# Longer estimated durations for the attention's matmuls, and a smaller allowance for array-mode changes, in the list schedule of an attention and MoE kernel on one Trainium2 core

## The chip, the cores and the metric

One core of one Trainium2 chip runs the whole kernel. The metric is the device time of one execution in microseconds, the median of several runs. Beside those runs there is one profiled execution, from which the trace comes.

## The reference

```
q_d, k_d, v_d = means over 4 neighbouring positions of q, k, v     # [4, 8, 144, 64] each
out_d     = softmax(q_d k_d^T / 8) v_d                             # coarse, global
out_up    = repeat(out_d, 4, axis=positions)
out_local = softmax(mask(q k^T / 8, |i - j| < 4)) v                # q, k, v: [4, 8, 576, 64]
x   = (out_up + out_local) as [2304, 512]
h   = x @ w_in                                                     # [512, 1024]
s   = h * softmax(h)
ln  = (s - mean(s)) / sqrt(var(s) + 1e-6) * g
x   = ln @ w_out                                                   # [1024, 512]
h2  = x @ w2_in                                                    # [512, 2048]
out = (h2 * cos(h2)) @ w2_out                                      # [2048, 512]
```

## The kernel before

The work falls into three parts that overlap. **Attention** goes over 4 batches, each in blocks of 192 positions and pairs of heads. The local part (class Loc) masks and scores with `ls` (L590 the mask, L592 the scores, three of 70 columns), makes a softmax (L475 to L482, the exponential L478 on ScalarE), transposes with `lt` (L600), copies on ScalarE (L602), and multiplies with the values, `lv` (L613, twelve small products for one block, 64 columns of the array wide). The global part (Glob) does the same on pooled positions: `gs` (L537, 64 rows by 64 columns of the array), `gt` (L548), `gv` (L559, 64 columns wide). **The first MoE layer** takes 128 tokens at a time: `h` is a product over w_in (h1_half), its maximum is L644, L655 to L659 make the softmax product and thereby free the bank of h, and ln_t transposes with `lnT` (L679) before x2 multiplies with w_out into `x`. **The second layer** has a plain start (plain_h, plain_o, 256 tokens) and then four groups of 512 tokens (quad_h, quad_o) by a Strassen-like scheme of seven products for each m from 0 to 7, into the banks s1, s26, s57 and s34; the names with numbers, as s26_6096, are those of one m (s26_5991 is m = 4, s26_6096 m = 5, s26_6201 m = 6, s26_6306 m = 7 of the first group; their cosines work in a_6041, a_6146, a_6251 and a_6356). VectorE sums the products (L981 to L988), the cosine runs through ScalarE and VectorE (L871, L873, L875, L876, L878), and its split into two parts (L387 hi on ScalarE, L388 lo on VectorE) gives GR, with which PE makes `oa` and `ob`.

All large products are made of three f32r products (mm3, L395 to L397) of a number split in a high and a low part by split (L387, L388). Four of the seven products of each m (the S products; the other three are plain) need S_h and S_l, sums of quarters of w2_in. combine(m) builds them in two half steps, each through the same buffer: a load from DRAM (L886), four sums on VectorE (L888 to L891), and a split, L387 on ScalarE to S_h and L388 on VectorE to S_l. w2o_step and wload bring the other weights; loads are issued by SP.

What sets the order is not the code's order. Each instruction is recorded as a Step with an estimated duration (Step.estimate, L110), connect finds what depends on what, and arrange (L201) makes a list schedule for all engines: forwards simulates the engines with these durations and takes at each turn the ready step with the earliest due time, backwards sets due times from the result, and of 20 rounds the order with the earliest estimated end is kept and fixed on every engine's queue. MODE_SWITCH (L50) is added on PE where the next matmul uses another width of the array than the last (Step.mode, L121); pick may also take a step of the same mode that is due up to PATIENCE later. 100 idle matmuls (L718) are due never, so they stand where the plan sees nothing else ready on PE.

Of the kernel before, what the change touches and what calls it, by code (L numbers as in the profile page):

```python
# [46 lines left out]
WRITTEN = {"DVE": 127.0, "Activation": 143.0, "Pool": 127.0}  # L47
DMA_ISSUE, DMA_START, DMA_END, DMA_RATE, DMA_FLIGHT = 475.0, 1100.0, 935.0, 250.0, 8
CLOCK_TICK, CLOCK_COLUMNS = 10240 / 3, 3060.0
MODE_SWITCH, PATIENCE = 150.0, 1200.0  # L50
NEVER = 1e18


# [18 lines left out]
def columns(o):  # L72
    n = 1
    for _, c in list(o.ap)[1:]:
        n *= c
    return n


def width(o):
    return next(z for b, z in (("64", 8), ("32", 4), ("16", 2), ("8", 1)) if b in str(o.dtype))  # L80
# [18 lines left out]
class Step:  # L99
# [10 lines left out]
    def estimate(self, psum):  # L110
        out, n, kind = self.outs[0], columns(self.outs[0]), self.x.opcode
        if self.dma:
            self.bytes = n * list(out.ap)[0][1] * width(out)
            return DMA_START + self.bytes / DMA_RATE + DMA_END
        wide = max([n] + [columns(o) for o in self.ins[:1]])
        if self.engine == "PE":
            d = str(self.ins[0].dtype)
            passes = 1 if "float32r" in d or "bf" in d else 2 if n == 128 else 4
            self.count = passes * n * list(self.ins[0].ap)[0][1] / 128

            self.mode = tuple(64 if list(o.ap)[0][1] <= 64 else 128 for o in (self.ins[0], out))  # L121
            if "float32r" in d:
                return 11.0 + 0.426 * max(n, 256)
            if self.mode[1] == 64:

                return 2.0 + 0.65 * max(n, 60)
            return 5.0 + passes * n / 2.4
        if self.engine == "Activation":
            at = 52 if self.ins[0].bass_ap.tensor.name in psum else 94
            return at + 0.833 * wide + (186 if len(self.outs) > 1 else 0)  # L130
        if self.engine == "DVE":
            full = [o for o in self.ins if columns(o) == n]
            if "TensorScalar" in kind and len(full) == 1 and n >= 256:
                return 65 + 0.535 * n + (110 if len(self.ins) > 1 else 0)
            return 65 + 1.045 * wide
        if self.engine == "Pool":
            return 464 if wide == 1 else 245 + (1.73 if kind == "TensorTensor" else 3.4 if "Ptr" in kind else 0.4) * wide
        return 60.0
# [943 lines left out]
```

## Time and profile before

| | us |
|---|---|
| median of 3 runs | 777.99 (777.79 to 779.13) |
| the profiled execution | 776.28 |
| its span, first to last instruction | 774.5 |
| PE busy (matmuls) | 751.2 |
| VectorE (DVE) busy | 625.7 |
| ScalarE (ACT) busy | 453.2 |

PE is TensorE, PEld its loading of weights, DVE is VectorE, ACT ScalarE, POOL GpSimd, SPq the queue on which SP issues transfers. A time at the start of a row counts from the first instruction of the span. A busy time of PE holds modelled ends, so the spacing of two matmuls is read from their starts. One score (L592) and one product of lv, gs or gv leave two records each in the trace; a transpose and an f32r product leave one.

### The profile page before, as it was taken

The page shows a single profiled execution, that of the slowest core. Times are in us where ns is not written, and L with a number is a line of the kernel's source. Part 1 is how long each engine was busy: PE and PEld are TensorE (multiplying, and loading weights), DVE is VectorE, ACT ScalarE, POOL GpSimd, SP SyncE. Part 2 cuts the span into 40 slices and gives each one's busy share as a digit, 9 for nine tenths or more (in the row PEclk, how much of TensorE's full clock was granted, in tenths as well). Part 3 has the DMA queues.
Part 4 walks back from the last instruction along what each step waited for, and adds up shares of the span by engine and source line. Part 5 has one row for each costly group of instructions (what it writes and reads, how often), then busy time and mean ns, then how long its engine had stood idle before and what let it go on. Part 6 is the DMA issues. An engine that isn't in the chain of part 4 may idle for free.

```text
span 774.5 us, 14770 instructions
## 1 busy us (share of the span) xinstructions
PE 751.2 (97%) x5444; PEld 648.6 (84%) x5444; DVE 625.7 (81%) x1435; ACT 453.2 (59%) x1060; POOL 19.3 (2%) x38
## 2 busy tenths in 40 slices
PE   6999999999999999999999999799999999999998
PEld 4667688888879788888988898698898889888896
DVE  5999999999886778889688998877678677787673
ACT  2656776646663735545567665565557565566544
POOL 3000000000100000000000000000000000000000
PEclk9999999999999999999999999999999999999999
DMA  9998655486763225556553533223211331113201
GB/s 249 275 250 239 190 154 164 130 218 187 224 207 126 75 77 162 159 163 199 187 139 101 154 110 95 69 69 123 69 41 48 130 94 44 41 54 110 55 28 55
DMA packets 82168, 101.85 MB, mean 132 GB/s; under 512 B 26128, under 2 KB 55088, under 8 KB 82096
## 3 DMA queue, kind: packets, MB, share of 16 engines
q1 hardware_dynamic: 82096, 100.91, 44.7%
q8 instruction: 43, 0.70, 0.4%
q14 instruction: 29, 0.24, 0.1%
HBM read 83.58 MB, written 17.30 MB: 130 GB/s over the span
## 4 chain that ended last, share of the span: by engine, by line
PE 69%; DVE 17%; DMA 6%; ACT 4%; issue 2%; POOL 1%; SPq 0%; POOLq 0%; DVEq 0%; ACTq 0%
PE s L395 5%; PE s L397 5%; PE s L396 5%; PE ls L592 3%; PE h L395 3%; PE h L396 3%; PE h L397 3%; PE x L395 3%; PE x L396 3%; PE oa L397 3%; PE x L397 3%; PE oa L395 3%; PE ob L395 3%; PE oa L396 3%; PE ob L396 3%; PE ob L397 3%
## 5 line engine op out<-in xcount | busy, mean ns | idle before, releaser
L395 PE MATMUL x<-P,R 128*128 128x256 f32 x288 | 81.2, 285 | 1.0 <-ACT P L387 0.6
L396 PE MATMUL x<-P,R 128*128 128x256 f32 x288 | 81.2, 283 | 0.5 <-DVE P L388 0.3
L397 PE MATMUL x<-P,R 128*128 128x256 f32 x288 | 80.9, 283 | 0.0
L395 PE MATMUL s<-R 128*128 128x256 f32 x256 | 71.5, 284 | 1.4 <-ACT R L387 1.0
L396 PE MATMUL s<-R 128*128 128x256 f32 x256 | 71.6, 282 | 0.5 <-DVE R L388 0.5
L397 PE MATMUL s<-R,S_l 128*128 128x256 f32 x256 | 70.9, 282 | 0.0
L395 PE MATMUL h<-R,P 128*128 128x512 f32 x144 | 60.7, 421 | 1.2 <-DVE e L659 1.2
L397 PE MATMUL h<-R,P 128*128 128x512 f32 x144 | 59.7, 415 | 0.0
L396 PE MATMUL h<-R,P 128*128 128x512 f32 x144 | 59.3, 412 | 0.1
L478 ACT ACTIVATE le<-ls,sm 128x70 f32<-128x70 f32 x144 | 44.2, 319 | 23.9 <-DVE X L616 8.1
L395 PEld LDWEIGHTS x<-P,R 128*128 128x128 f32 x288 | 54.0, 188 | 2.3 <-ACT P L387 1.4
L396 PEld LDWEIGHTS x<-P,R 128*128 128x128 f32 x288 | 54.1, 188 | 1.4 <-DVE P L388 1.1
L397 PEld LDWEIGHTS x<-P,R 128*128 128x128 f32 x288 | 54.0, 188 | 0.3
L396 PE MATMUL s<-R,w2i 128*128 128x256 f32 x192 | 54.0, 282 | 0.0
L397 PE MATMUL s<-R,w2i 128*128 128x256 f32 x192 | 53.9, 281 | 0.0
L395 PE MATMUL s<-R,w2i 128*128 128x256 f32 x192 | 53.8, 282 | 0.0
L387 ACT ACTIVATE GR<-a 128x1024 fp32r<-128x1024 f32 (+1 forms) x40 | 39.1, 978 | 21.0 <-DVE a L878 20.9
L395 PEld LDWEIGHTS s<-R 128*128 128x128 f32 x256 | 48.0, 189 | 3.1 <-ACT R L387 1.6
L875 ACT ACTIVATE a<-a 128x1024 f32<-128x1024 f32 (+1 forms) x40 | 38.9, 972 | 19.8 <-DVE a L873 19.6
L396 PEld LDWEIGHTS s<-R 128*128 128x128 f32 x256 | 48.6, 190 | 1.6 <-DVE R L388 0.9
L397 PEld LDWEIGHTS s<-R,S_l 128*128 128x128 f32 x256 | 48.2, 190 | 0.2
L388 DVE TENSOR_TENSOR GR<-a,GR 128x1024 fp32r<-128x1024 f32 (+1 forms) x40 | 44.6, 1114 | 2.8 <-ACT GR L387 2.4
(167 smaller groups left out, 2200.0 us busy)
## 6 DMA issues: line engine op xcount, KB each, us to landing
wo<-drw SPq DMA_DIRECT2D x80, 256.0 KB
X<-in_w2o_dram SPq DMA_DIRECT2D x32, 256.0 KB
wr<-in_w2i_dram SPq DMA_DIRECT2D x32, 256.0 KB
lv<-in_vl_dram SPq DMA_DIRECT2D x48, 105.0 KB
kt<-in_k_dram SPq DMA_DIRECT2D x8, 594.0 KB
kw<-in_k_dram SPq DMA_DIRECT2D x24, 198.0 KB
qt<-in_q_dram SPq DMA_DIRECT2D x8, 576.0 KB
diag<-in_q_dram SPq DMA_DIRECT2D x48, 96.0 KB
```

What stands on the lines that cost most here:

```text
L387: nc.scalar.activation(out=hi, in_=src, func=AF.Copy)
L388: nc.vector.tensor_tensor(out=lo, in0=src, in1=hi.bitcast(F32), op=ALU.subtract)
L395: nc.tensor.matmul(ps, lh, rh, start=start, stop=False)
L396: nc.tensor.matmul(ps, lh, rl, start=False, stop=False)
L397: nc.tensor.matmul(ps, ll, rh, start=False, stop=stop)
L478: nc.scalar.activation(out=e[:, j, :], in_=src[:, j, :], func=AF.Exp, bias=neg[:, j:j + 1], scale=scale, accum_out=ssum[:, j:j + 1])
L592: nc.tensor.matmul(ps[:, a * WIN:(a + 1) * WIN], self.d["q"][:, self.h, a].rearrange("p j s -> p (j s)"), self.d["k"][:, self.h, a * QB:a ...
L875: nc.scalar.activation(out=a, in_=a, func=AF.Sin, scale=0.5)
```

## The change

Two estimates of arrange's plan are replaced, and one is split in two; no computation, tile or buffer changes. A product on 64 columns of the array (lv, gs, gv) is estimated at 20 + 0.83 n ns instead of 2 + 0.65 n, with n columns moved and 60 at least. Every other matmul that isn't float32r keeps its estimate where it is bf16; a float32 one is estimated at passes / 2 times the larger of 110 and 3 + n / 1.2 ns, instead of 5 + passes x n / 2.4 (passes is 2 for n = 128, so for the transposes, and 4 else, so for the scores). And the allowance for a change of mode goes from 150 to 80 ns.

```
-MODE_SWITCH, PATIENCE = 150.0, 1200.0
+MODE_SWITCH, PATIENCE = 80, 1200.0
...
             if self.mode[1] == 64:

-                return 2.0 + 0.65 * max(n, 60)
-            return 5.0 + passes * n / 2.4
+                return 20.0 + 0.83 * max(n, 60)
+            if "bf" in d:
+                return 5.0 + n / 2.4
+            return passes / 2 * max(110.0, 3.0 + n / 1.2)
```

In the orders of the changed kernel every line above 128 of the file is two higher (L397 there is L395 before).

PE, in the first MoE layer, the transposes lnT of a_t and the attention around them; before:

```order
L397 MATMUL h_3301<-R_75,P 128x512
L679 MATMUL lnT<-ident,e 128x128 x8
L613 MATMUL lv<-at,lv 64x64 x11
L590 LDWEIGHTS identb
L590 MATMUL ls<-mask,identb 128x210
L592 MATMUL ls<-kw,diag_112 128x70 x3
```

and after:

```order
L399 MATMUL h_3301<-R_75,P 128x512
L681 MATMUL lnT<-ident,e 128x128 x3
L561 MATMUL gv<-at,gvs 64x144 x4
L550 MATMUL gt<-ident,ge 72x128 x3
L681 MATMUL lnT<-ident,e 128x128 x2
L550 MATMUL gt<-ident,ge 72x128 x3
L681 MATMUL lnT<-ident,e 128x128 x3
L592 LDWEIGHTS identb
L592 MATMUL ls<-mask,identb 128x210
L594 MATMUL ls<-kw,diag_112 128x70 x3
```

The eight transposes were in one piece with lv behind them; now gv and gt stand among them, and lv is elsewhere.

VectorE (DVE), in the second layer, the cosine of m = 4 (a_6041), the sums of m = 5 (s26_6096 and following, into hs) and a half step of the combination (the sums of wr with wr, and S_l); before:

```order
L388 TENSOR_TENSOR GR_5112<-a_6041,GR_5112 128x1024
L388 TENSOR_TENSOR w2i10_3926<-wo_6192,w2i10_3926 128x512
L981 TENSOR_TENSOR hs_5113<-s26_6096,hs_5113 128x512
L888 TENSOR_TENSOR wr_3928<-wr_3928 128x128
L889 TENSOR_TENSOR wr_3928<-wr_3928 128x128
L890 TENSOR_TENSOR wr_3928<-wr_3928 128x128
L984 TENSOR_TENSOR hs_5113<-s57_6097,hs_5113 128x512
L891 TENSOR_TENSOR wr_3928<-wr_3928 128x128
L985 TENSOR_TENSOR hs_5113<-s57_6097,hs_5113 128x256
L988 TENSOR_TENSOR hs_5113<-s34_6098,hs_5113 128x512
L388 TENSOR_TENSOR S_l_5111<-wr_3928,R1_75 128x4x128
L873 SCALAR_TENSOR_TENSOR a_6146<-a_6146,hs_5113 128x1024
```

and after:

```order
L890 TENSOR_TENSOR wr_3928<-wr_3928 128x128
L891 TENSOR_TENSOR wr_3928<-wr_3928 128x128
L892 TENSOR_TENSOR wr_3928<-wr_3928 128x128
L390 TENSOR_TENSOR w2i10_3926<-wo_6091,w2i10_3926 128x512
L893 TENSOR_TENSOR wr_3928<-wr_3928 128x128
L880 SCALAR_TENSOR_TENSOR a_6041<-a_6041,wr_3928 128x1024
L390 TENSOR_TENSOR S_l_5111<-wr_3928,R1_75 128x4x128
L983 TENSOR_TENSOR hs_5113<-s26_6096,hs_5113 128x512
L390 TENSOR_TENSOR GR_5112<-a_6041,GR_5112 128x1024
L986 TENSOR_TENSOR hs_5113<-s57_6097,hs_5113 128x512
L390 TENSOR_TENSOR w2i10_3926<-wo_6192,w2i10_3926 128x512
L987 TENSOR_TENSOR hs_5113<-s57_6097,hs_5113 128x256
```

The half step, which began behind the GR of m = 4 and ended behind the last sum of m = 5, now ends ahead of both that GR and the first sum of m = 5.

## Rows read from the trace of the kernel before

**Rows 1.** The page, part 1: busy us (share of the span) and instructions.

```profile
PE 751.2 (97%) x5444; PEld 648.6 (84%) x5444; DVE 625.7 (81%) x1435; ACT 453.2 (59%) x1060; POOL 19.3 (2%) x38
```

**Rows 2.** Stages: length, busy PE, PEld, DVE, ACT, POOL, granted clock, DMA.

```profile
60.00:100.00 40.00, 37.31 (x289) 28.36 (x288) 37.86 (x115) 27.70 (x99) 1.11 (x2) 0.96 0.75 218
180.00:380.00 200.00, 196.21 (x1575) 173.92 (x1574) 160.54 (x495) 106.61 (x317) 9.39 (x12) 1.00 0.51 156
380.00:480.00 100.00, 98.47 (x610) 86.21 (x610) 88.59 (x163) 66.75 (x105) 0.00 (x0) 1.00 0.43 126
480.00:505.00 25.00, 20.73 (x116) 17.82 (x115) 19.52 (x34) 13.94 (x20) 0.00 (x0) 0.93 0.21 64
```

**Rows 3.** Timeline of PE, 255 to 257 us: start, duration, engine, line, what.

```profile
255.35 0.80 PE L592 MATMUL ls<-kw,diag 128*128 128x70 f32 x6
255.96 0.48 PE L396 MATMUL h<-R,P 128*128 128x512 f32 x1
256.28 0.39 PE L397 MATMUL h<-R,P 128*128 128x512 f32 x1
256.51 0.40 PE L395 MATMUL h<-R,P 128*128 128x512 f32 x1
256.84 0.92 PE L613 MATMUL lv<-at,lv 70*64 70x64 f32 x24
```

**Rows 4.** The same from 257.62 us: the last six of those 24 records.

```profile
257.41 0.34 PE L613 MATMUL lv<-at,lv 70*64 70x64 f32 x6
257.69 0.26 PE L590 MATMUL ls<-mask,identb 128*128 128x210 bf16 x1
```

**Rows 5.** Timeline of PE at 250 and at 292 us.

```profile
250.21 1.03 PE L679 MATMUL lnT<-ident,e 128*128 128x128 f32 x8
251.08 0.25 PE L590 MATMUL ls<-mask,identb 128*128 128x210 bf16 x1
...
291.59 1.03 PE L679 MATMUL lnT<-ident,e 128*128 128x128 f32 x8
292.38 0.48 PE L395 MATMUL h<-R,P 128*128 128x512 f32 x1
```

**Rows 6.** Waits of PE, 0 to 310 us: total us, times, longest.

```profile
PE ls L590 <- ACT ge L478: 1.6, 2, 1.0
...
PE h L395 <- DVE e L659: 1.2, 2, 0.6
...
PE ls L590 <- ACT le L478: 0.4, 1, 0.4
```

**Rows 7.** Timeline of DVE, 478 to 503 us; in brackets the idle time before.

```profile
479.49 0.68 DVE L388 TENSOR_TENSOR S_l<-wr,R 128x512 fp32r<-128x512 f32 x1
...
483.14 0.29 DVE L888 TENSOR_TENSOR wr<-wr 128x128 f32<-128x128 f32 x1 [1.15 <-DMA wr<-dra]
...
486.55 0.69 DVE L388 TENSOR_TENSOR w2i<-wo,w2i 128x512 fp32r<-128x512 f32 x1
487.15 0.68 DVE L981 TENSOR_TENSOR wr<-s,wr 128x512 f32<-128x512 f32 x1
487.75 1.22 DVE L388 TENSOR_TENSOR GR<-a,GR 128x1024 fp32r<-128x1024 f32 x1
...
493.55 1.23 DVE L873 SCALAR_TENSOR_TENSOR a<-a,wr 128x1024 f32<-128x1024 int32 x1 [0.93 <-ACT a L871]
...
497.37 1.23 DVE L878 SCALAR_TENSOR_TENSOR a<-a,wr 128x1024 f32<-128x1024 f32 x1 [0.25 <-ACT a L876]
```

**Rows 8.** Timeline of PE, 495 to 504 us.

```profile
496.04 0.28 PE L396 MATMUL s<-R 128*128 128x256 f32 x1
496.16 0.28 PE L397 MATMUL s<-R,S_l 128*128 128x256 f32 x1
499.74 0.54 PE L395 MATMUL oa<-w2i,GR 128*128 128x512 f32 x1 [3.30 <-ACT GR L387]
500.08 0.63 PE L396 MATMUL oa<-w2i,GR 128*128 128x512 f32 x1
500.50 0.63 PE L395 MATMUL oa<-w2i,GR 128*128 128x512 f32 x1
```

## The prediction

> **What bounds the kernel now.** I read the page first, then a table by stage, then the waits, and last the start times where the waits lie. The page shows PE busy for 97% of the span [rows 1]. PE's own work is the bound on the whole, and a new order can win only three things: what PE loses between instructions of different kinds, the few microseconds in which it waits, and stretches at half clock. The stages say where these lie [rows 2]: PE idles 2.69 us from 60 to 100 us, 3.79 from 180 to 380, 1.53 from 380 to 480, and 4.27 us in only 25 us from 480 to 505. From there on the order of every engine soon becomes the same row by row, so nothing is to be had later. VectorE is full from 60 to 100 us (37.86 of 40) and next to it from 380 to 480 (88.59 of 100): where PE waits there, it waits for a chain that runs through VectorE.
>
> **What the change does to the estimates.** Three scores (L592) take from 255.35 to 255.96 us [rows 3], 0.20 us each; the old estimate was 122 ns, the new one is 220. There are 144 of them, so the old plan believed PE some 14 us freer in the attention (144 x 0.098) than the new one does. The first nine of twelve products of L613 start within 0.57 us (256.84 to 257.41) [rows 3, 4], 0.063 each; the old estimate was 44 ns, the new one 73, so the error only changes sign. The allowance: two h products start 0.23 us apart (256.28 to 256.51), and from an h to the first L613 it is 0.33 [rows 3], so entering costs 0.10. Leaving: the last three products start at 257.41, the next instruction at 257.69 [rows 4]; at 0.063 each that leaves 0.09. I take 0.095 for a change either way. 80 ns is nearer to it than 150, a little low.
>
> **Term 1, PE's own order: slower by 1.6 us.** The instructions are the same ones, 100 idle matmuls among them. Counted over the whole order, changes of array width between neighbouring matmuls go from 142 to 152: 10 x 0.095 = +0.95 us. A second thing moves that the plan does not price. Eight transposes of lnT followed by a mask product take 0.87 us to the next start (250.21 to 251.08), and followed by an h product 0.79 (291.59 to 292.38) [rows 5]: a float32 transpose that ends against an f32r product gives 0.08 us back. Such ends (of lnT, lt and gt) go from 64 to 57: 7 x 0.08 = +0.56. Scores that end against an f32r product go from 24 to 22, under 0.1 us. The sum is +1.6, and as PE is full, nothing covers it. Bounds: changes of width at 0.08 give +1.4, at 0.13 +1.9.
>
> The Trainium skill (TensorEngine Tiling (Array Packing), Key Properties) says that a change of the tiling mode drains TensorE. The trace agrees in kind: rows 3 show a loss at the change. The skill's page TensorE: Matmul & The Clock Gate (Single matmul latency) puts the fixed part of one matmul at about 0.17 us; ten changes at that price would be an estimated 1.7 us instead of 0.95, and the sum 0.75 us slower.
>
> **Term 2, the attention's waits: 2.0 us back.** Up to 310 us PE waits 2.0 us in all with a mask product (L590), whose bank a softmax (L478) has not left yet, and 1.2 us for L659 to free the h bank [rows 6]. The first follows from the estimates: scores believed half as long are planned in front of a softmax that in truth is not finished. I take those 2.0 us off. Bounds: nothing (they move elsewhere), and 3.2 with the L659 wait too. I leave that one in, since the first L659 is row 154 of VectorE's order before and row 154 after, at about 62 us, where VectorE is full.
>
> **Term 3, the combination of w2i: 1.6 us back.** From about 383 to 502 us VectorE and ScalarE build S_h and S_l in sixteen half steps through one buffer: a reload (L886), four sums (L888 to L891), a copy on ScalarE (L387), a rest on VectorE (L388, S_l), and only then the next reload. PE needs them in order. In the trace the S_l of the first half for m = 6 starts at 479.49, and L888 of the second half at 483.14, after 1.15 us idle for the reload [rows 7]: a half step wants 3.65 us from one start to the other. Before, only one L873 lies between. After, that S_l stands ahead of L981 of m = 5, and between it and the next L888 lie L981, a GR, L984, a split and L985. With 0.6 us from start to start for S_l, L981, L984 and the split, as 486.55 to 487.15 and to 487.75 show, 1.2 for the GR by its row and 0.4 for the half as wide L985, that is 4.0 us [rows 7]. So the 1.15 us go. The L873 of m = 6 waited 0.93 us for ScalarE [rows 7], and has a GR and an S_l between L988 and itself now (1.8 us): 0.9 go. Its L878 waited 0.25 [rows 7] and has more splits ahead of it, but part of a half step too: 0.25 go, and two rows of about 0.35, 0.7, come on. 1.15 + 0.9 + 0.25 - 0.7 = 1.6 us by which the GR of m = 6 comes earlier. PE starts its last product at 496.16 and is let go by that GR at 499.74, after 3.30 us idle [rows 8]; it has nothing else to run, so what the GR gains PE gains. Bounds: nothing, and the whole 3.3 us.
>
> **Term 4, the clock: nothing taken.** The mean granted clock is 0.96 over the 40 us from 60 and 0.93 over the 25 us from 480 [rows 2]; as the clock has two levels, 1.2 and 2.4 GHz, that is some 3.3 us at half clock each time, after PE had waited. At half clock a product of 512 columns starts every 0.42 us (500.08 to 500.50) [rows 8], at full clock every 0.23 [rows 3]; some seven a stretch, 7 x 0.19 = 1.3 us, 2.6 for both. A wait of 3.30 us stands ahead of the second, one of 1.0 [rows 6] is the longest near the first; by term 3 some 1.7 us are left of the former, between the two. I leave both stretches in and keep 2.6 us for the lower end.
>
> **Sum:** +1.6 - 2.0 - 1.6 = -2.0 us. The profiled execution takes 776.28 us, of which 774.5 are the span; the median of the three runs is 777.99, 1.7 us above it. I put the difference on the median: **776.0 us**. A measurement of this kernel can tell about 0.2%, 1.6 us, from no change, so the forecast lies just beyond that on the fast side.
>
> **Rivals.**
> - *More goes than waits* (23%): the waits shrink far enough that the clock does not fall either. -2.0 - 2.6 = -4.6, 773.4 us. For it: both falls come right behind waits that the change touches. Against: the first also stands behind L659, which does not move.
> - *The waits only change place* (24%): PE pays the 1.6 us of term 1 and gets nothing back. 779.6 us, at the border of what can be told. For it: VectorE is full where PE waits, and its sum of work is the same in both orders; and PE, better planned or not, waits for the same loads.
> - *Slower, by the cosine of m = 4* (12%). For the combination to go forward something on VectorE goes back. Ahead of the GR of m = 4 (a_6041) stand now, beyond what stood there, one half step and L981 of m = 5: 4 x 0.3 + 0.6 + 0.6 = 2.4 us by [rows 7]. If PE comes to the oa products of m = 4 as early as before, it waits these 2.4 us: 1.6 + 2.4 = +4.0, 782.0 us. It decides if PE's other products do not last; seventeen S products and six plain ones of m = 5 (23 x 0.12 = 2.8 us, by 496.04 to 496.16 in [rows 8]) have moved ahead of those oa products, which would just cover it.
> - *The change does nothing* (5%): gains and losses cancel, 778.0 us.
>
> **How the numbers follow.** The forecast has 36%. Its own range, 1.4 us to either side of 776.0, crosses the bound of 0.2% at 776.4: 22% faster, 14% no change. The first rival is faster (23%); the second falls on the bound at 779.6, 11% no change and 13% slower; the third is slower (12%); the last is no change (5%). Together 45% faster, 30% no change, 25% slower. The range for 8 in 10 goes from 772.0 (the first rival, with the upper bound of term 2 on top) to 781.0 (the second with a microsecond of the third; the third itself is left out).
>
> **What would show it.** Term 1: as many idle matmuls, and PE's busy time up by one or two microseconds. Term 2: the waits of L590 for L478 under 1 us. Term 3: the wait of L888 for the reload under 1 us from 478 to 505 us, and the wait of oa for GR near 1.7. Term 4: two stretches at half clock again. I am wrong if PE waits for the GR of m = 4, or if a wait longer than 1.5 us comes up between 60 and 310 us, where no part of this sum has one.

## The result and the profile after

The changed kernel takes 772.51 us (median of 8 runs, 769.33 to 775.33) where the kernel before takes 778.52 beside it (8 runs, 777.75 to 780.46): ratio 0.9919, 95% interval 0.9893 to 0.9944. It is faster by 6.0 us; the forecast was 2.0. The profiled execution after takes 771.89 us with a span of 770.1, so between the two profiled executions 4.4 us of the span went.

First the page, part 1, of the kernel after, which answers to [rows 1]:

```profile
PE 749.4 (97%) x5444; PEld 646.9 (84%) x5444; DVE 625.4 (81%) x1435; ACT 454.5 (59%) x1060; POOL 18.7 (2%) x38
```

The instructions are as many as before, and PE's busy time is 1.8 us less, though the order holds more changes of array width: matmuls at half clock are busy for longer (0.63 us in [rows 8] against 0.40 in [rows 3]), and they are fewer. The table by stage of the kernel after shows it (length, busy PE, PEld, DVE, ACT, POOL, granted clock, DMA):

```profile
60.00:100.00 40.00, 39.44 (x314) 29.83 (x312) 39.93 (x122) 27.53 (x102) 1.11 (x2) 1.00 0.92 225
...
480.00:505.00 25.00, 23.39 (x134) 19.86 (x133) 22.24 (x39) 17.04 (x24) 0.00 (x0) 1.00 0.20 58
```

Against [rows 2], PE idles 0.56 us from 60 to 100 us where it idled 2.69, and 1.61 from 480 to 505 where it idled 4.27; both falls of the granted clock (0.96 and 0.93) have become 1.00. The waits of PE over the whole span after (total us, times, longest):

```profile
PE oa L397 <- ACT GR L389: 3.4, 5, 1.6
PE gs L539 <- ACT le L480: 1.4, 1, 1.4
...
PE lt L602 <- DVE X L618: 1.3, 2, 1.0
PE x L398 <- DVE P L390: 0.9, 1, 0.9
PE s L397 <- ACT R L389: 0.8, 1, 0.8
...
PE ls L592 <- ACT ge L480: 0.7, 1, 0.7
PE lv L615 <- ACT at L604: 0.4, 1, 0.4
PE x L397 <- ACT P L389: 0.3, 1, 0.3
PE lt L602 <- DVE le L484: 0.2, 1, 0.2
```

The mask product's waits for softmaxes, 2.0 us in all in [rows 6], are 0.7. The longest waits of a `gs` and an `lt` are 1.4 and 1.0 instead. The waits of `oa` and `s` lie in the second layer, all the others shown here ahead of it. Now the place of term 3. PE after, 495 to 498 us, answers to [rows 8]:

```profile
495.05 0.28 PE L399 MATMUL s<-R,S_l 128*128 128x256 f32 x1
496.93 0.50 PE L397 MATMUL oa<-w2i,GR 128*128 128x512 f32 x1 [1.61 <-ACT GR L389]
497.27 0.39 PE L398 MATMUL oa<-w2i,GR 128*128 128x512 f32 x1
497.50 0.40 PE L397 MATMUL oa<-w2i,GR 128*128 128x512 f32 x1
```

PE waits 1.61 us for the GR of m = 6 instead of 3.30, and the products behind it start 0.23 us apart, at full clock, where before they started 0.42 apart. VectorE after, 474 to 495 us, answers to [rows 7]:

```profile
474.69 0.68 DVE L390 TENSOR_TENSOR S_l<-wr,R 128x512 fp32r<-128x512 f32 x1
...
478.58 0.28 DVE L890 TENSOR_TENSOR wr<-wr 128x128 f32<-128x128 f32 x1
...
490.15 1.22 DVE L875 SCALAR_TENSOR_TENSOR a<-a,wr 128x1024 f32<-128x1024 int32 x1
...
494.48 1.22 DVE L880 SCALAR_TENSOR_TENSOR a<-a,wr 128x1024 f32<-128x1024 f32 x1
```

From that S_l to the next half step's first sum pass 3.89 us without idle time (the forecast added up 4.0), and the two cosine steps of m = 6, which had waited 0.93 and 0.25 us, wait for nothing.

**Two numbers for each run.** In the experiments I count PE's matmul instructions from the first h2a product on, where the attention is over, and cut at the 701st (471.50 us before, 471.56 after). "Early" is the start of that instruction, "late" the time from there to the start of PE's last one. Early holds all of the attention, the first layer and the start of the second, with the first stretch of term 4; late holds the place of term 3 and the second stretch of term 4. The cut counts instructions, and orders differ in what they have done by then: priced at 0.23 and 0.12 us for products of 512 and 256 columns, what is left behind the cut is the same within 0.1 us for most of these kernels, but 0.7 to 0.9 us less than the change's for the allowances 95, 160 and 140 and for the scores' line alone. Each number is from one profiled execution, whose own time stands beside it. The ratio compares all runs and isn't the quotient of the two medians.

| kernel | median us, before beside it | ratio, 95% interval | profiled | early | late |
|---|---|---|---|---|---|
| before | 778.52 | | 776.28 | 471.5 | 298.8 |
| the change | 772.51, 778.52 | 0.9919 [0.9893, 0.9944] | 771.89 | 471.6 | 294.4 |
| the change's order again | 773.21, 778.47 | 0.9930 [0.9906, 0.9953] | 774.62 | 473.6 | 295.1 |
| durations only | 779.53, 777.29 | 1.0042 [1.0010, 1.0073] | 783.76 | 479.5 | 298.4 |
| allowance only | 785.65, 777.29 | 1.0120 [1.0084, 1.0156] | 785.20 | 480.0 | 299.2 |
| before's order, then the change's | 778.35, 777.29 | 1.0016 [0.9996, 1.0036] | 776.84 | 476.4 | 294.4 |
| the change's order, then before's | 777.09, 777.29 | 1.0023 [0.9994, 1.0051] | 775.99 | 471.6 | 298.4 |
| before's, the change's from 421 us | 775.49, 778.47 | 0.9965 [0.9943, 0.9987] | 776.45 | 476.1 | 294.3 |
| allowance 90 | 772.44, 778.47 | 0.9923 [0.9898, 0.9948] | 772.44 | 471.6 | 294.9 |
| allowance 95, other 64-column line | 770.72, 778.47 | 0.9909 [0.9879, 0.9939] | 777.87 | 478.6 | 293.3 |
| allowance 120 | 776.98, 777.89 | 0.9998 [0.9970, 1.0026] | 775.35 | 471.3 | 298.1 |
| allowance 160 | 776.34, 777.89 | 0.9984 [0.9962, 1.0005] | 773.91 | 474.4 | 293.5 |
| scores' line alone, allowance 80 | 776.22, 777.89 | 0.9978 [0.9959, 0.9996] | 776.47 | 476.7 | 293.8 |
| before with allowance 140 | 778.12, 777.89 | 1.0016 [0.9991, 1.0040] | 777.55 | 475.8 | 295.8 |

Between the profiled executions of before and after, early is the same (0.1 us apart) and late is 4.4 us shorter: all of the difference between these two spans lies behind 471 us.

### The profile page after: what moved, and what is told of

Read it like the earlier page. It is cut to its first block, busy times and chain, and to the rows that moved or that the text cites. A ratio compares the mean times of both kernels' runs of the same rounds, so it can differ in the third digit from the quotient of the medians.

```text
span 770.1 us, 14778 instructions
## 1 busy us (share of the span) xinstructions
PE 749.4 (97%) x5444; PEld 646.9 (84%) x5444; DVE 625.4 (81%) x1435; ACT 454.5 (59%) x1060; POOL 18.7 (2%) x38
## 4 chain that ended last, share of the span: by engine, by line
PE 54%; DVE 28%; DMA 8%; ACT 4%; issue 4%; POOL 1%; SPq 0%; POOLq 0%; DVEq 0%; ACTq 0%
PE s L399 6%; PE s L397 6%; PE s L398 6%; PE oa L397 3%; PE oa L399 3%; PE ob L397 3%; PE ob L399 3%; PE ob L398 3%; PE oa L398 3%; DMA wr<-in_w2i_dram 3%; DVE P L390 3%; DMA wr<-dra 2%; PE ls L594 2%; PE idle L720 2%; DVE e L661 2%
## 5 line engine op out<-in xcount | busy, mean ns | idle before, releaser
L397 PE MATMUL x<-P,R 128*128 128x256 f32 x288 | 81.1, 285 | 0.4 <-ACT P L389 0.3
L397 PE MATMUL s<-R 128*128 128x256 f32 x256 | 71.3, 283 | 0.0
L397 PE MATMUL h<-R,P 128*128 128x512 f32 x144 | 60.4, 419 | 0.1
L398 PE MATMUL h<-R,P 128*128 128x512 f32 x144 | 58.7, 408 | 0.0
L399 PE MATMUL h<-R,P 128*128 128x512 f32 x144 | 58.4, 406 | 0.0
L397 PEld LDWEIGHTS x<-P,R 128*128 128x128 f32 x288 | 54.1, 188 | 1.8 <-ACT P L389 1.2
L397 PE MATMUL s<-R,w2i 128*128 128x256 f32 x192 | 53.9, 282 | 0.8 <-ACT R L389 0.8
L389 ACT ACTIVATE GR<-a 128x1024 fp32r<-128x1024 f32 (+1 forms) x40 | 39.1, 977 | 22.4 <-DVE a L880 22.3
L397 PEld LDWEIGHTS s<-R 128*128 128x128 f32 x256 | 47.8, 188 | 1.2 <-ACT R L389 0.3
L390 DVE TENSOR_TENSOR GR<-a,GR 128x1024 fp32r<-128x1024 f32 (+1 forms) x40 | 44.6, 1115 | 3.9 <-ACT GR L389 3.7
```

The lines of the kernel that those rows point to most:

```text
L389: nc.scalar.activation(out=hi, in_=src, func=AF.Copy)
L390: nc.vector.tensor_tensor(out=lo, in0=src, in1=hi.bitcast(F32), op=ALU.subtract)
L397: nc.tensor.matmul(ps, lh, rh, start=start, stop=False)
L398: nc.tensor.matmul(ps, lh, rl, start=False, stop=False)
L399: nc.tensor.matmul(ps, ll, rh, start=False, stop=stop)
```

## The experiments

**One edit without the other.** The new durations with the old allowance:

```
-MODE_SWITCH, PATIENCE = 80, 1200.0
+MODE_SWITCH, PATIENCE = 150.0, 1200.0
```

> The new durations with the old allowance of 150 ns for a change of mode. Theory (the corrected durations make the gain, through fewer waits of PE in the attention and an earlier combination of w2i): 4 to 7 us faster than before, about 772.5, two of the changed kernel's 6 us at most missing. Rival A (the smaller allowance makes it): within 1.6 us of before. Rival B (any other order of this plan lands a few microseconds from the old one, whatever the numbers mean): anywhere from 6 faster to 3 slower, with no relation to the other three runs.

And the old durations with the new allowance, an edit of the kernel before:

```
-MODE_SWITCH, PATIENCE = 150.0, 1200.0
+MODE_SWITCH, PATIENCE = 80.0, 1200.0
```

> The allowance of 80 ns alone, with the old durations; the order has 153 changes of array width against 142. Theory: within 1.6 us of before, on the slower side, since the eleven more changes cost 11 x 0.095 = 1.0 us and no wait is planned better. Rival A (the allowance makes the gain): 4 to 7 us faster. Rival B (any other order): anywhere from 6 faster to 3 slower.

Measured: 2.2 us and 8.4 us slower by the medians. The first lies outside the theory and rival A and within rival B's range; the second is outside all three. Neither edit brings the gain by itself, so it can't be shared out between them. In the run with the durations alone PE waits once for 3.62 us in late, and the clock falls behind it. PE, 503 to 508 us:

```profile
503.65 0.28 PE L399 MATMUL s<-R,S_l 128*128 128x256 f32 x1
507.55 0.58 PE L397 MATMUL s<-R 128*128 128x256 f32 x1 [3.62 <-ACT R L389]
507.93 0.42 PE L398 MATMUL s<-R 128*128 128x256 f32 x1
508.14 0.42 PE L397 MATMUL s<-R 128*128 128x256 f32 x1
```

The R it waits for is the combination's S_h, by ScalarE of the same run:

```profile
506.87 0.63 ACT L389 ACTIVATE R<-wr 128x512 fp32r<-128x512 f32 x1
```

In the run with the allowance alone late is what it was before, and early is 8.5 us longer, the same as the medians' 8.4. Its PE waits, 50 to 110 us, then the row of the second wait, and then its table by stage:

```profile
PE ls L590 <- ACT ge L478: 1.8, 1, 1.8
PE gt L548 <- ACT at L549: 1.3, 1, 1.3
```

```profile
92.79 0.41 PE L548 MATMUL gt<-ident,ge 128*72 128x128 f32 x2 [1.34 <-ACT at L549]
```

```profile
93.00:107.00 14.00, 13.79 (x71) 9.82 (x70) 10.01 (x28) 7.12 (x20) 0.55 (x1) 0.51 0.58 163
```

Two waits, 3.1 us together, are followed by stretches at half clock, one of them nearly all of 93 to 107 us. Priced at full-clock spacing, the matmuls of early lose an estimated 7 us in such stretches, so the clock costs more here than the waits before it.

**Half of one order with half of the other.** Both plans are made, and each engine's queue takes the first plan's order up to a mark and the second's behind it:

```
+    steps, kept, at = plan(tc, pools, reopened, True)
+    _, kept2, _ = plan(tc, pools, reopened, False)
+    mark = next(s for s in steps if s.engine == "PE" and s.outs[0].bass_ap.tensor.name.startswith("h2a"))
+    early = {s.at for s in steps if at[s] < at[mark]}
...
+        order = [s for s in kept[e] if s.at in early]
+        order += [steps[s.at] for s in kept2[e] if s.at not in early]
```

`plan` is arrange up to its kept order; its last argument chooses the old durations and allowance. Lines of the mixed kernels are 15 higher than the change's (L412 is L397, L404 is L389). As printed, before's order runs to the first h2a product, and the change's from there.

> The order of before up to the first product of the second layer, from there on the order of the change, on every engine. In the two profiles the change is 0.75 us ahead at that product (361.14 to 360.39 us) and 4.4 us ahead at the end. Theory (most of the gain is the combination of w2i moved forward on VectorE): 3 to 4 us faster than before, no stretch at half clock near 500 us. Rival C (the second part is faster only because the first part hands over earlier or with other loads in flight): within 1.6 us of before.

Measured: no change that can be told, and late 294.4, the change's own. Early is lengthened at the seam, where neither plan would have stood so: PE, 362 to 368 us:

```profile
362.52 0.28 PE L412 MATMUL h2a<-R,w2i 128*128 128x256 f32 x1
366.60 0.80 PE L412 MATMUL x<-P,R 128*128 128x256 f32 x2 [3.80 <-ACT P L404]
367.19 0.41 PE L413 MATMUL h2a<-R,w2i 128*128 128x256 f32 x1
367.41 0.41 PE L414 MATMUL h2a<-R,w2i 128*128 128x256 f32 x1
```

The 3.80 us and the half clock behind them hide the gain; the median says nothing on the theory, the late column does. The other way round (`True` and `False` exchanged), the change's order runs to the first h2a product and before's follows:

> The order of the change up to the first product of the second layer, from there on the order of before. Theory: about 1 us faster than before, the wait of PE for a GR at about 499 us of 3 us and the half clock behind it are back. Rival C (the first part makes the gain, by what it hands over): 4 us or more faster, without that wait.

Measured: no change that can be told. Early is the change's own, and late is back at 298.4 with the wait and the half clock. PE, 496 to 502 us:

```profile
496.37 0.28 PE L414 MATMUL s<-R,S_l 128*128 128x256 f32 x1
499.90 0.79 PE L412 MATMUL oa<-w2i,GR 128*128 128x512 f32 x1 [3.25 <-ACT GR L404]
500.49 0.63 PE L413 MATMUL oa<-w2i,GR 128*128 128x512 f32 x1
500.92 0.63 PE L412 MATMUL oa<-w2i,GR 128*128 128x512 f32 x1
```

So the change's order of the attention gives nothing that can be measured when before's second layer follows it. The third mix puts the mark at the first s1 product, at about 421 us, away from that seam:

```
-    mark = next(s for s in steps if s.engine == "PE" and s.outs[0].bass_ap.tensor.name.startswith("h2a"))
+    mark = next(s for s in steps if s.engine == "PE" and s.outs[0].bass_ap.tensor.name.startswith("s1"))
```

> The order of before up to the first product of the Strassen-like groups (about 421 us), from there the order of the change. The earlier cut at the first product of the second layer left a seam: PE waited 3.8 us for a split of x2 there and ran at half clock for 6.8 us behind it, which hides what the second part is worth. Theory (the combination of w2i moved forward on VectorE is most of the gain): no such seam, the wait for the GR near 499 us falls from 3.3 to 1.6 us as in the change, no half clock there; 2.5 to 4 us faster than before. Rival C (the second part is faster only by what the first hands over): within 1.6 us of before, with the wait of 3 us.

Measured: 2.7 us faster by the ratio, late 294.3. PE, 499 to 502 us:

```profile
499.61 0.28 PE L414 MATMUL s<-R,S_l 128*128 128x256 f32 x1
501.41 0.50 PE L412 MATMUL oa<-w2i,GR 128*128 128x512 f32 x1 [1.51 <-ACT GR L404]
501.74 0.40 PE L413 MATMUL oa<-w2i,GR 128*128 128x512 f32 x1
501.98 0.39 PE L412 MATMUL oa<-w2i,GR 128*128 128x512 f32 x1
```

With the change's order from 421 us on, the wait is the short one, the clock stays up there, and the kernel is faster than before with before's own attention ahead, though by the ratio it gains less than half of what the change does. The same program text with the change's plan on both sides of the mark (both last arguments `False`) gives the change's order, as a second measurement of it:

> The order of the change on every engine, instruction by instruction, made by the same two-plan code as the other mixed kernels: a second measurement of the change, beside the kernels of this call. Theory (the change itself is worth 4 to 6 us): 4 to 7 us faster than before. If the first comparison was favoured by what else ran: within 2 us of before.

Measured: ratio 0.9930. The result repeats; early of one and the same order is 2.0 us apart in the two profiled executions, so early can't be read more closely than that.

**Neighbouring numbers.** An allowance nearer to the measured 95 ns, and both numbers as I would take them from the trace:

```
-MODE_SWITCH, PATIENCE = 80, 1200.0
+MODE_SWITCH, PATIENCE = 90, 1200.0
```

> The new durations with an allowance of 90 ns instead of 80, which nothing in the traces tells apart from it; some 500 of 4986 rows of PE stand elsewhere. Theory (the figures are right, so the gain is broad): within 2 us of the change. Rival B (any order of this plan lands a few microseconds from the next): 2 us or more away from the change, either way.

```
-MODE_SWITCH, PATIENCE = 80, 1200.0
+MODE_SWITCH, PATIENCE = 95, 1200.0
...
-                return 20.0 + 0.83 * max(n, 60)
+                return 15.0 + 0.74 * max(n, 60)
```

> The figures that the trace of before gives: 95 ns for a change of width, and 15 + 0.74 n ns for products on 64 columns (62 for 64 columns, 122 for 144), scores as in the change. Theory (truer figures make better plans): as fast as the change or up to 2 us faster. Rival B: no better than the others, anywhere from 6 us faster than before to 8 slower, and decided in the first 360 us by waits of 1 to 4 us and by half clock behind them.

Measured: 0.9923 and 0.9909, both as fast as the change within their intervals. The first is close kin: by their place in the traces, 461 of PE's 5444 records differ from the change's, against 2072 for the second. The second has the shortest late of all (0.8 us of it by where the cut falls), and no wait for a GR there; its PE waits from 478 us on are one row:

```profile
PE s L397 <- ACT R L389: 0.7, 1, 0.7
```

Its profiled execution is the slowest of its runs (777.87; the others have 769.22 to 776.91), so its early isn't typical.

After these three (80, 90, 95, all near 0.992) it looked as if a true allowance was what mattered. Four more orders tested that. The change with an allowance of 120, and with 160:

```
-MODE_SWITCH, PATIENCE = 80, 1200.0
+MODE_SWITCH, PATIENCE = 120, 1200.0
```

> The change's durations with an allowance of 120 ns. 148 changes of width (152 in the change, 142 with the allowance at 150). On VectorE the half step's S_l of the second layer stands next to the first sum of m = 5, as in the change and unlike before. Theory A, the time gets worse steadily as the allowance leaves the measured 95 ns: half way between the change and the run at 150, ratio 0.997 to 1.000. Theory B, the attention's order is a draw each time and only the combination's place can be told from the order: from the first h2a product to the last PE start 405 to 407 us, as in the change; the first 360 us anywhere from 359 to 371, so a ratio from 0.990 to 1.005, with no order among the allowances.

```
-MODE_SWITCH, PATIENCE = 80, 1200.0
+MODE_SWITCH, PATIENCE = 160, 1200.0
```

> The change's durations with an allowance of 160 ns. 147 changes of width; the same place of the half step as in the run at 120. Theory A, worse steadily with the allowance: not faster than the run at 150, ratio 1.003 or more. Theory B, a draw in the attention: second part 405 to 407 us, and a ratio anywhere from 0.990 to 1.010; a ratio under 0.998 here speaks against A.

Measured: 0.9998 and 0.9984. At 160 the kernel is faster than at 150 (1.0042, the intervals don't touch), so the time doesn't get steadily worse with the allowance: theory A falls. Theory B's number for the second part came out at 120 (405.7 us from the first h2a product to the last) and was missed at 160 (404.4, shorter still). At 120 its reason did not come out. There the half step stands early and PE waits all the same, by the waits from 470 to 505 us:

```profile
PE oa L397 <- ACT GR L389: 3.7, 2, 2.3
```

It is the GR's time that counts, and the place of one half step doesn't settle it. Then the change with one of its two new durations:

```
-                return 20.0 + 0.83 * max(n, 60)
+                return 2.0 + 0.65 * max(n, 60)
```

> The change without its line for 64 columns: the longer estimate for float32 matmuls (scores, transposes) alone and the allowance of 80 ns. 139 changes of width. If the scores' estimate is what the gain in the attention needs, the mask product's waits stay under 1 us together and the ratio is 0.990 to 0.994, as with the change. If both lines are needed, these waits or others of 1 to 2 us come back and the ratio is 0.997 or more. The half step stands early here too, so the second part is 405 to 407 us by either.

Measured: 0.9978, and the mask's waits are back. PE waits, 50 to 110 us:

```profile
PE ls L592 <- ACT le L480: 2.0, 2, 1.0
PE h L397 <- ACT R L389: 1.9, 1, 1.9
```

Late is as short as the change's (293.8), early 5.1 us longer. The scores' estimate alone doesn't take these waits away. Last, the kernel before with an allowance of 140:

```
-MODE_SWITCH, PATIENCE = 150.0, 1200.0
+MODE_SWITCH, PATIENCE = 140.0, 1200.0
```

> The kernel before with an allowance of 140 ns instead of 150 and the old durations: a small step that means nothing for the plan's truth, but gives another order. 142 changes of width, as before; the half step of the combination stands early, beside the first sum of m = 5. Theory of the combination: the second part is 405 to 407 us, 2 to 4 shorter than before. Theory of a draw: the first 360 us are 358 to 371, ratio 0.994 to 1.010. If the old durations cost something by themselves, the mask product (L590) waits 1.5 us or more for softmaxes, as before.

Measured: no change that can be told. Late is 295.8, 3.0 shorter than before (from the first h2a product to the last it is 405.4 us where before has 409.2), with the old durations; early is 4.3 longer and eats it up. A short late is to be had without any of the change's numbers, then. And the mask product waits for no softmax here, so the old durations by themselves don't bring those waits.

## Why the prediction was right and where it was off

The sign and the range held (its lower end is 772.2 by its own sum, the upper one 780.6; 772.0 and 781.0 were stated). The size was 2.0 us for a measured 6.0, 4.4 by the profiled executions. *More goes than waits*, at 773.4, came nearest.

**Terms 1 and 2** (+1.6 and -2.0, so -0.4 up to the second layer): the first h2a product starts 0.75 us earlier (361.14 to 360.39), but by other parts, so it is luck that the sum looks right. The mask's waits fell from 2.0 to 0.7 us, and the 1.2 us for L659, which the forecast left in, went too. Other waits took their place. These are before's waits up to the second layer that [rows 6] leaves out, save those for the mask itself at the very start, which are the same in both kernels:

```profile
PE x L395 <- ACT P L387: 0.6, 1, 0.6
PE gv L559 <- ACT at L549: 0.5, 1, 0.5
...
PE gs L537 <- ACT le L478: 0.4, 1, 0.4
PE x L396 <- DVE P L388: 0.3, 1, 0.3
...
PE gt L548 <- ACT g L562: 0.2, 1, 0.2
```

With those of [rows 6] they add up to 5.2 us; the rows of the kernel after, shown above, add up to 5.2 as well. So term 2 brought nothing. Its reason isn't borne out either: with the scores' new estimate alone the mask waits 2.0 us, and with the old one and an allowance of 140 not at all. What did come is the first stretch at half clock, before:

```profile
63.12 0.59 PE L396 MATMUL h<-R,P 128*128 128x512 f32 x1
...
66.78 0.39 PE L396 MATMUL h<-R,P 128*128 128x512 f32 x1
```

Nine products take 3.66 us there, and 2.1 at full clock: 1.6 us. Only 0.75 of them are left at the first h2a product, so some 0.8 us are lost elsewhere, which is all that remains for term 1 and everything else. Before's order alone starts that product at 361.14, 359.54 and 362.95 us in three profiled executions (before and two of the mixes), so term 1 is neither shown nor refuted. Its sign in PE's busy time did not come: that is 1.8 us lower, since I had left the clock out of it. That the order of the attention bought nothing measurable with before's second layer behind it is shown by the mix (1.0023).

**Term 3** (-1.6, from -3.3 to 0) had its mechanism right, and for the wait it named its size too: PE's wait for the GR of m = 6 fell from 3.30 to 1.61 us, 1.69, where the forecast left some 1.7. It missed a second wait that hangs on the same half steps. PE needs their S_h too, which ScalarE copies behind the fourth sum. Before, PE and ScalarE at 485 us:

```profile
485.61 0.38 PE L395 MATMUL s<-R 128*128 128x256 f32 x1 [0.98 <-ACT R L387]
```

```profile
484.93 0.63 ACT L387 ACTIVATE R<-wr 128x512 fp32r<-128x512 f32 x1 [0.37 <-DVE wr L891]
```

After, that copy stands earlier, and PE doesn't wait for it:

```profile
481.11 0.62 ACT L389 ACTIVATE R<-wr 128x512 fp32r<-128x512 f32 x1
```

That is another 1.0 us, and I had followed the half steps to the GR only.

**Term 4, the clock, is the step that failed.** I took nothing, because 1.7 us of wait would be left, between a wait behind which the clock had fallen (3.30) and one of 1.0. Both stretches went. The first is priced above, at 1.6 us. The second ends before this row of the kernel before:

```profile
503.49 0.28 PE L396 MATMUL s<-R 128*128 128x256 f32 x1
```

From 500.08 us [rows 8] to this start are six products of 512 columns and four of 256, 3.41 us where they take 1.9 at full clock: 1.5 us, and 3.1 for both stretches where the forecast priced 2.6. Late shrank by 4.4 us: 1.7 of the GR's wait, 1.0 of the S_h, 1.5 of the clock, and the 0.2 left are about what PE waited for another GR at 474.27 (0.25 us). The mixes show the wait and the clock together twice: with 3.25 us of wait the products behind start 0.43 apart, with 1.51 us 0.24 apart. So the wait and the clock behind it should have been one term, -1.6 - 1.0 - 1.5, with the clock's part hanging on how much wait is left.

The clock also tells where most of the 6.0 us lies, since the mean granted clock is on record for runs without a trace too. For the second measurement of the change its mean is 0.9989 over 8 runs, for the kernel before beside it 0.9938 over 26: some 1.7 and 9.7 us at half clock a run. At 1.5 us lost for each 3.4 that is an estimated 3 to 3.5 of the 5.3 us between the medians, as some of it lies at the very end, where it costs nothing. What is left, some 2, is near the forecast's 2.0, which had no clock in it, though by other parts.

The **rivals**: slower by the cosine of m = 4 did not come; PE waits for nothing from 470 to 482 us, where that GR (L390 at 475.90) lets its products go. No wait over 1.5 us came up between 60 and 310 us. That the waits only change place is true up to the second layer (5.2 us in both) and false behind it.

**What stays open.** The median of the change is 6.0 us lower and the profiled executions show 4.4: before's profiled execution is 2.2 us below its median, the change's 0.6. So some 1.6 us of the gain lie in what these two executions don't show. The two halves don't add up either: by the ratios, the change's order up to the first h2a product alone costs 1.8 us, not to be told from nothing, and from 421 us alone it gains 2.7, while the whole gains 6.3, or 5.4 in the second measurement. Some 4 to 5 us, roughly, since each ratio has an interval of about 2 us to either side, need both halves together or the change's order between these two marks, which neither mix has. No run tells which. Nor do the runs show whether truer durations pay in general. By the ratios, of the allowances with the change's durations 80 and 90 gain some 6 us, 120 and 160 at most what can just be told, and 150 loses 3; of those with the old durations 140 changes nothing and 80 loses 9. Early goes from 471 to 480 us over these orders; where a trace was followed, by waits of 1 to 3 us and the clock behind them, and in part by what differs from one execution to the next. With so few independent orders, that the change's numbers are nearer to the trace and that its order is a lucky one can't be told apart.

No order that ran beats the change by more than its interval; the one with an allowance of 95 and 15 + 0.74 n (770.72 us, 0.9909) is as good.

## What to carry to other kernels

A change of a planner's costs gives another order, and its worth is read from the few places where the bound engine waits: follow each late step to everything that hangs on it (here both halves of one sum), and price a wait together with the clock behind it. An estimate that is nearer to the truth is no gain by itself: one allowance, moved alone from 150 to 80, cost 8.4 us. When such a change pays, run its neighbours before crediting the numbers, and cut the program where the work has one order, so that two parts of a run can be compared with many others.

## What the runs showed that was not expected

- In the second layer, half clock came behind each wait of 3.25 to 3.80 us (five of these kernels), and not behind 1.51, 1.61 or 2.3. In the attention it came behind less: before, behind two waits of 1.0 and 0.6 us ahead of 63 us; in the run with the allowance alone, PE waited 1.34 us at 92.79 and the granted clock was 0.51 from 93 to 107. The wait's length alone doesn't tell it.
- Short waits can cost more than themselves: in that run two waits of 3.1 us together stand from 50 to 110 us, and an estimated 7 us are lost at half clock in early.
- Profiled executions of one order differ by 2.4 us (the change's) and 3.4 us (before's) at the first h2a product, and by 0.7 in late, so a term of 2 us in the attention can't be proved by one profile.
